# LayerNorm scaling of 32 token blocks moved from GpSimd to VectorE, with smaller presets, in a transformer layer whose engine queues a planner orders

## The chip, the core and the metric

The kernel runs on one core of one Trainium2 chip. The core's engines work in parallel, each through its own queue, strictly in order: TensorE (PE: matmul, with its weight load shown as PEld), VectorE (DVE), ScalarE (ACT), GpSimd (POOL) and SyncE (SP, which here only issues DMAs). An instruction starts when all semaphores that it waits for have come and the instruction ahead of it on its engine has gone. The metric is the device time of one execution in microseconds (us); lower is better.

## The reference

One pre-LayerNorm layer on 2048 tokens of 448 features, in bfloat16. Attention looks back at 8 positions two apart; the second half is a gated MLP in which tokens are mixed by a 2048 by 2048 matrix.

```python
def _A_ref(x, wqkv, wo):                 # 16 heads of 28, window 8, dilation 2
    q, k, v = split(x @ wqkv)
    idx = pos[:, None] - arange(8) * 2   # earlier positions; idx < 0 is masked
    attn = softmax(where(mask, q . k[idx] * 28 ** -0.5, -1e9))
    return (attn . v[idx]).reshape(B, S, D) @ wo
def _B_ref(x, w_in, w_sp, b_sp, w_out):
    z = gelu(x @ w_in)                   # 1792 wide
    z1, z2 = z[..., :896], layernorm(z[..., 896:])
    g = einsum('ts,bsf->btf', w_sp, z2) + b_sp
    return (z1 * g) @ w_out
h  = x + _A_ref(layernorm(x), wqkv, wo)
h2 = h + _B_ref(layernorm(h), w_in, w_sp, b_sp, w_out)
```

## The kernel before

The work is a graph of small tasks. A task names an engine (or two to choose from), an assumed duration in us, the buffers that it reads and writes, and a priority. `Graph.schedule` runs a list scheduler over the graph when the kernel is built: it always takes the engine that can start a ready task soonest, and there the task of the best priority. What comes out is a fixed order for each engine's queue; `Sched` then adds the semaphore waits. So an assumed duration never delays anything on the chip by itself. It decides where a task stands in its queue, and on which of two engines a copy out of PSUM lands.

Tokens are handled in 16 blocks of 128 (`m`); attention in 18 blocks of 114 queries (`i`). The stages that matter here:

- `layernorm(m, 0)` for the 16 blocks of x, and `layernorm(m, 1)` for the 16 blocks of h: DVE takes statistics (`bn_stats` L486, `bn_aggr` L488), POOL makes the reciprocal deviation in two one-column instructions (`va`, L512, and the power `rstd`, L514, both in `rstd_of`), POOL scales the 128x448 block into the ring `tring` (L491), PE transposes it with four matmuls (L496), and ACT or DVE copies the result into `xhT` (L508 or L509, both in `copy_on`).
- `qk_tile`: query and key projections, 32 tiles of four matmuls (L524). `att_block`: V projection (L535), logits (L547), exponential on ACT (L556), mask on DVE (L564), attention times V (L569), normalisation on DVE (L575, L577), transposition (L582). `y_block`: output projection (L596) and residual add on DVE (L599).
- The MLP: z2 tiles (L632), their GELU (ACT, L637), a LayerNorm of 896 columns with statistics and scaling on DVE (L640, L642, L645) and `rstd_of` on POOL; then z1 tiles (L654), the token mixing (L667) and the output (L685).

At the start POOL presets constants: the ring `V1` (4 slots, L424), whose column 28 of each head has to hold 1, and the ring `E` (3 slots, L426), whose columns past the queries are read by L569. POOL also copies the key weights (L475), PE runs 28 warm-up matmuls (L479), and DVE makes the attention mask (L429 to L434).

Of the kernel before, what the change touches and what calls it, by code (L numbers as in the profile page):

```python
# [9 lines left out]
DH = 28  # L10
F_DIM = 1792
FH = 896
EPS = 1e-5
# [4 lines left out]
NQ = 114  # L18
# [6 lines left out]
F32 = mybir.dt.float32  # L25
I32 = mybir.dt.int32
ALU = mybir.AluOpType
# [270 lines left out]
def bass_sequential_preLN__sliding_local_dilated__mixer_gmlp__prompt_kernel(  # L298
# [13 lines left out]
    G = Graph()  # L312

    with contextlib.ExitStack() as top:
        def sb(name, shape, dt):
            return top.enter_context(nc.sbuf_tensor(name, shape, dt))

        NTR, NST, NV, NE, NOT, NU = 4, 4, 4, 3, 2, 3
        x_tm = sb("x_tm", [128, NB, D], BF16)
        tring = sb("tring", [128, NTR, D], BF16)  # L320
# [5 lines left out]
        mhalf = sb("mhalf", [128, 1], F32)  # L326
        st = sb("st", [128, NST, 12], F32)
        mv = sb("mv", [128, 3 * NB, 2], F32)
        va = sb("va", [128, 3 * NB], F32)
        rstd = sb("rstd", [128, 3 * NB], F32)  # L330
# [11 lines left out]
        V1 = sb("V1", [128, NV, NHEAD, 32], BF16)  # L342
        E = sb("E", [128, NE, NHEAD, 128], BF16)
# [32 lines left out]
        P_V = Pool("V", NV)  # L376
        P_E = Pool("E", NE)
# [12 lines left out]
        def act_us(n, sbuf=False):  # L390
            return (n + (190 if sbuf else 105)) / 1200.0

        def dve_us(n, rate=1.0):
            return (n / rate + 85) / 960.0
# [4 lines left out]
        def blocks_of(lo, hi):  # L399
# [12 lines left out]
              writes=r_wq, prio=-95)  # L412
        G.add([("pool", 0.2)], [lambda e: e.memset(wkp.rearrange("p c g (h d) -> p (c g h) d", h=4)[:, :, 28:32], 0.0)],
              writes=r_wk, prio=-94)
# [6 lines left out]
                                                          channel_multiplier=1)], reads=[r_mf], writes=[r_mf], prio=-50)  # L421
        G.add([("pool", 0.2)], [lambda e: e.iota(ij, [[1, 128]], base=0, channel_multiplier=1)], writes=[r_ij], prio=-50)
        for s in range(NV):
            G.add([("pool", 0.5)], [lambda e, s=s: e.memset(V1[:, s], 1.0)], writes=[P_V.res[s]], prio=-40)  # L424
        for s in range(NE):
            G.add([("pool", 0.9)], [lambda e, s=s: e.memset(E[:, s].bitcast(F32), 0.0)], writes=[P_E.res[s]], prio=-40)  # L426
        init_slots = {P_V: [P_V.res[s].w_task for s in range(NV)], P_E: [P_E.res[s].w_task for s in range(NE)]}
        for fn, rd, wr in (
            (lambda e: e.tensor_single_scalar(ij, ij, 1, ALU.bitwise_and), [r_ij], [r_ij]),  # L429
# [52 lines left out]
        def layernorm(m, i, prio):  # L482

            k = i * NB + m
            s = Buf(P_st)
            G.add([("dve", dve_us(D))], [lambda e: e.bn_stats(st[:, s.slot, 0:6], x_tm[:, m, :])],  # L486
                  [r_x[m]], [s], [s], prio=prio)
            G.add([("dve", 0.10)], [lambda e: e.bn_aggr(mv[:, k, :], st[:, s.slot, 0:6])], [s], [r_mv[k]], prio=prio)  # L488
            rstd_of(k, prio)
            t = Buf(P_tr)  # L490
            G.add([("pool", 0.65)], [lambda e: e.tensor_scalar(tring[:, t.slot, :], x_tm[:, m, :], mv[:, k, 0:1],  # L491
                                                              rstd[:, k:k + 1], ALU.subtract, ALU.mult)],
                  [r_x[m], r_mv[k], r_rs[k]], [t], [t], prio=prio)
            b = Buf(P_bank)
            G.add([("pe", 0.27)], [
                lambda e, c=c: e.transpose(psb[0:DC, b.slot * 1024 + c * 128: b.slot * 1024 + c * 128 + 128],  # L496
                                           tring[:, t.slot, c * DC:(c + 1) * DC], ident[:, :]) for c in range(NCH)],
                [t, r_ident], [b], [b], prio=prio)

            def evac(e):  # L500
                dst = xhT[0:DC, :, PAD + 128 * m: PAD + 128 * m + 128]
                src = psb[0:DC, b.slot * 1024: b.slot * 1024 + 512].rearrange("p (c t) -> p c t", c=NCH)
                return copy_on(e, dst, src)
            G.add([("act", act_us(512)), ("dve", dve_us(512, 2))], [evac], [b], [r_xhT[m]], prio=prio)

        def copy_on(e, dst, src):
            if hasattr(e, "activation"):
                return e.activation(dst, src, AF.Copy)  # L508
            return e.tensor_copy(dst, src)  # L509

        def rstd_of(k, prio):
            G.add([("pool", 0.2)], [lambda e: e.tensor_scalar(va[:, k:k + 1], mv[:, k, 1:2], EPS, None, ALU.add)],  # L512
                  [r_mv[k]], [r_va[k]], prio=prio)
            G.add([("pool", 0.3)], [lambda e: e.tensor_tensor(rstd[:, k:k + 1], va[:, k:k + 1], mhalf[:, 0:1], ALU.pow)],  # L514
                  [r_va[k], r_half], [r_rs[k]], prio=prio)

        def qk_tile(tc, g8, prio):
# [12 lines left out]
        def att_block(i):  # L530
# [23 lines left out]
            for hh in range(4):  # L554
# [10 lines left out]
                                          maskb[0:nk, mi:mi + 1, 0:nq].to_broadcast([nk, NHEAD, nq]), ALU.mult)],  # L565
                [ev, r_mask], [ev], prio=i - 0.6)
            ob = Buf(P_bank)
            G.add([("pe", 0.9)], [
                lambda e, g=g, hh=hh: e.matmul(psum[:, ob.slot * 512 + (4 * g + hh) * 32: ob.slot * 512 + (4 * g + hh) * 32 + DH + 1],  # L569
                                               E[0:nk, ev.slot, hh * 4 + g, :], V1[0:nk, v.slot, 4 * g + hh, 0:DH + 1])  # L570
                for g in range(4) for hh in range(4)],
# [18 lines left out]
        def y_block(m):  # L590
            lo, hi = 128 * m, 128 * m + 128
            ro = [r_OT[b] for b in range(NAB) if _att_geom(b)[0] < hi and _att_geom(b)[0] + _att_geom(b)[1] > lo]
            b = Buf(P_bank)
            p = pos(m) + 1.6
            G.add([("pe", pe_us(4, D))], [
                lambda e, c=c: e.matmul(bank(b, D), qT[0:DC, c, PAD + lo:PAD + hi], wo_sb[:, c, :],  # L596
                                        start=(c == 0), stop=(c == NCH - 1)) for c in range(NCH)],
                ro + [r_wo], [b], [b], prio=p)
            G.add([("dve", dve_us(D))], [lambda e: e.tensor_tensor(x_tm[:, m, :], bank(b, D), x_tm[:, m, :], ALU.add)],  # L599
                  [b, r_x[m]], [r_x[m]], prio=p)  # L600
            layernorm(m, 1, p + 0.3)
# [6 lines left out]
        for m in range(NB):  # L608
            layernorm(m, 0, pos(m) - 7.0)
# [5 lines left out]
        for i in range(NAB):  # L615
            att_block(i)
            t0, nq, nk = _att_geom(i)
            while next_y < NB and (i == NAB - 1 or 128 * next_y + 128 <= t0 + nq - PAD):
                y_block(next_y)
                next_y += 1  # L620
# [4 lines left out]
        for m in range(NB):  # L625
            k = 2 * NB + m
            s = Buf(P_st)
# [129 lines left out]
```

## Time and profile before

| | |
|---|---|
| Time, median of 3 runs | 301.98 us (301.05 to 302.22) |
| The profiled execution: its own time, its span | 302.17 us, 300.5 us |
| PE busy, share of the span | 268.0 us, 89% |
| DVE busy | 153.1 us, 51% |
| ACT busy | 102.2 us, 34% |
| POOL busy | 111.9 us, 37% |
| Mean granted TensorE clock | 0.953 |

Busy time is the time in which an engine's instructions ran. Instructions of an engine overlap a little at their ends, so busy time can pass the time that went by. The span goes from the first to the last instruction that the profile shows; the time of an execution holds a little more than its span. The granted clock is a share of 2.4 GHz: 0.5 is 1.2 GHz throughout.

### The profile page before, as it was taken

What the parts mean: (1) busy time and instruction counts of PE and PEld (TensorE: products, weight loads), DVE (VectorE), ACT (ScalarE), POOL (GpSimd) and SP (SyncE); (2) the same over time, 40 slices, a digit from 0 to 9 for tenths busy, and PEclk for the clock granted to TensorE, in tenths of its full rate; (3) what the DMA queues carried; (4) which work ended last, traced back from release to release, by engine and by line L of the source; (5) the groups of instructions that cost most, each with busy time, mean ns of one, the idle gap of its engine ahead of it and who ended that gap; (6) DMA issues with size and microseconds to landing.
All of it is one profiled execution on the core that took longest, in us unless ns stands there. A gap on an engine that the chain in (4) does not pass through costs nothing.

```text
span 300.5 us, 4652 instructions
## 1 busy us (share of the span) xinstructions
PE 268.0 (89%) x1868; PEld 133.9 (45%) x1868; DVE 153.1 (51%) x321; ACT 102.2 (34%) x193; POOL 111.9 (37%) x155
## 2 busy tenths in 40 slices
PE   7489894997797869878999999999999999999995
PEld 2144452553463445534544444444444444444442
DVE  6861593693795767777996222322133122322223
ACT  1236773564684564545760110010100111011000
POOL 9999999858635353386443000000000000000000
PEclk9879998799999965899999999999999999999999
DMA  7999450000000001222200003443034520000001
GB/s 174 301 260 215 99 87 1 2 2 0 0 2 2 2 17 37 53 52 51 53 21 2 0 0 55 98 96 97 0 83 97 101 65 0 31 33 0 0 2 61
DMA packets 42182, 16.91 MB, mean 56 GB/s; under 512 B 35248, under 2 KB 41584, under 8 KB 42160
## 3 DMA queue, kind: packets, MB, share of 16 engines
q1 hardware_dynamic: 42160, 16.61, 23.7%
q8 instruction: 15, 0.25, 0.3%
q14 instruction: 7, 0.06, 0.1%
HBM read 6.37 MB, written 1.84 MB: 27 GB/s over the span
## 4 chain that ended last, share of the span: by engine, by line
PE 55%; POOL 29%; DVE 9%; DMA 2%; issue 2%; ACT 0%; DVEq 0%; SPq 0%; POOLq 0%
PE psum L667 31%; POOL tring L491 18%; POOL rstd L514 8%; PE psum L654 7%; PE psum L685 7%; POOL va L512 3%; PE psum L596 3%; DVE st L640 2%; PE psum L496 2%; DMA early<-in_A_wqkv_dram 2%; PE psum L524 2%; DVE z2p L645 2%; DVE st L486 1%; PE psum L547 1%; DVE x_tm L599 1%
## 5 line engine op out<-in xcount | busy, mean ns | idle before, releaser
L491 POOL TENSOR_SCALAR tring<-x_tm,mv,rstd 128x448 bf16<-128x448 bf16 x32 | 63.5, 1988 | 3.8 <-PE psum L496 2.8
L672 DVE TENSOR_TENSOR ub<-psum,bb 128x512 bf16<-128x512 f32 x28 | 19.4, 691 | 83.8 <-PE psum L667 83.8
L659 ACT ACTIVATE z1p<-psum 128x512 bf16<-128x512 f32 x28 | 16.7, 597 | 114.8 <-PE psum L654 114.8
L667 PE MATMUL psum<-wsp,z2p 128*128 128x512 bf16 x224 | 51.2, 379 | 0.5 <-DVE z2p L645 0.5
L667 PE MATMUL psum<-early,z2p 128*128 128x512 bf16 x224 | 50.8, 379 | 0.0
L556 ACT ACTIVATE E<-psum 128x456 bf16<-128x456 f32 (+1 forms) x72 | 34.4, 557 | 14.8 <-PE psum L547 14.7
L496 PE MATMUL psum<-ident,tring 128*112 128x128 bf16 x128 | 15.2, 250 | 25.3 <-POOL tring L491 25.3
L667 PEld LDWEIGHTS psum<-wsp,z2p 128*128 128x128 bf16 x224 | 21.8, 98 | 27.2 <-DVE z2p L645 0.9
L667 PEld LDWEIGHTS psum<-early,z2p 128*128 128x128 bf16 x224 | 21.9, 98 | 26.4
L524 PE MATMUL psum<-xhT,early 112*128 112x512 bf16 x128 | 31.1, 379 | 0.0
L514 POOL TENSOR_TENSOR rstd<-va,mhalf 128x1 f32<-128x1 f32 x48 | 28.8, 610 | 1.4
L654 PE MATMUL psum<-xhT,w_in 112*128 112x512 bf16 x112 | 28.8, 378 | 0.0
L512 POOL TENSOR_SCALAR va<-mv 128x1 f32<-128x1 f32 x48 | 11.1, 244 | 43.4 <-DVE mv L488 31.1
L496 PEld LDWEIGHTS psum<-ident,tring 128*112 128x112 bf16 x128 | 11.4, 149 | 33.8 <-POOL tring L491 32.0
L632 PE MATMUL psum<-w_in,xhT 112*128 112x448 bf16 x128 | 26.0, 360 | 0.0
L509 DVE COPY xhT<-psum 112x512 bf16<-112x512 bf16 x19 | 7.9, 420 | 28.3 <-PE psum L496 28.3
L685 PE MATMUL psum<-w_out,z1p 128*128 128x448 bf16 x112 | 21.8, 352 | 0.0
L637 ACT ACTIVATE z2p<-psum 128x448 bf16<-128x448 f32 x32 | 17.3, 543 | 10.9 <-PE psum L632 10.9
L564 DVE TENSOR_TENSOR E<-E,maskb 128x1824 bf16<-128x1824 bf16 (+1 forms) x18 | 19.6, 1094 | 0.3 <-ACT E L556 0.2
L486 DVE BATCH_NORM_STATS2 st<-x_tm 128x6 f32<-128x448 bf16 x32 | 18.9, 611 | 1.3 <-DMA x_tm<-in_A_x_dram 1.0
L535 PE MATMUL psum<-early,xhT 112*128 112x448 bf16 (+1 forms) x72 | 19.2, 404 | 0.0
L640 DVE BATCH_NORM_STATS2 st<-z2p 128x6 f32<-128x448 bf16 x32 | 17.9, 600 | 0.0
(59 smaller groups left out, 261.0 us busy)
## 6 DMA issues: line engine op xcount, KB each, us to landing
out_dram<-tring SPq DMA_DIRECT2D x16, 112.0 KB, 1.8
w_in<-in_B_w_in_dram SPq DMA_DIRECT2D x1, 1568.0 KB, 14.0
x_tm<-in_A_x_dram SPq DMA_DIRECT2D x1, 896.0 KB, 10.5
early<-in_A_wqkv_dram SPq DMA_DIRECT2D x1, 784.0 KB, 6.2
w_out<-in_B_w_out_dram SPq DMA_DIRECT2D x1, 784.0 KB, 14.6
bb<-in_B_b_sp_dram SPq DMA_DIRECT2D x1, 512.0 KB, 13.3
wsp<-in_B_w_sp_dram SPq DMA_TRANSPOSE x32, 2.8
early<-in_B_w_sp_dram SPq DMA_TRANSPOSE x32, 2.6
```

The lines of the kernel that those rows point to most:

```text
L486: G.add([("dve", dve_us(D))], [lambda e: e.bn_stats(st[:, s.slot, 0:6], x_tm[:, m, :])], [r_x[m]], [s], [s], prio=prio)
L491: G.add([("pool", 0.65)], [lambda e: e.tensor_scalar(tring[:, t.slot, :], x_tm[:, m, :], mv[:, k, 0:1], rstd[:, k:k + 1], ALU.subtract, AL ...
L496: lambda e, c=c: e.transpose(psb[0:DC, b.slot * 1024 + c * 128: b.slot * 1024 + c * 128 + 128], tring[:, t.slot, c * DC:(c + 1) * DC], ide ...
L512: G.add([("pool", 0.2)], [lambda e: e.tensor_scalar(va[:, k:k + 1], mv[:, k, 1:2], EPS, None, ALU.add)], [r_mv[k]], [r_va[k]], prio=prio)
L514: G.add([("pool", 0.3)], [lambda e: e.tensor_tensor(rstd[:, k:k + 1], va[:, k:k + 1], mhalf[:, 0:1], ALU.pow)], [r_va[k], r_half], [r_rs[k ...
L524: lambda e, c=c: e.matmul(bank(b, 512), wsrc[:, c, gg, :], xhT[0:DC, c, col0:col0 + 512], start=(c == 0), stop=(c == NCH - 1)) for c in ra ...
L556: lambda e, hh=hh: e.activation(E[0:nk, ev.slot, hh * 4:(hh + 1) * 4, 0:nq], bank(lb[hh], 512, 0, nk).rearrange("p (g c) -> p g c", c=128) ...
L632: lambda e, c=c, b=b, h=h, m=m: e.matmul(bank(b, D), xhT[0:DC, c, PAD + 128 * m: PAD + 128 * m + 128], w_in[:, c, FH + D * h: FH + D * (h ...
L640: lambda e, h=h, m=m, s=s: e.bn_stats(st[:, s.slot, 6 * h:6 * h + 6], z2p[:, m, D * h:D * (h + 1)])],
L654: lambda e, c=c: e.matmul(bank(b, 512), w_in[:, c, fc * 128:(fc + 1) * 128], xhT[0:DC, c, PAD + 512 * tc: PAD + 512 * (tc + 1)], start=(c ...
L667: lambda e, s=s: e.matmul(bank(b, 512), z2p[:, s, fc * 128:(fc + 1) * 128], w[:, s, :], start=(s == 0), stop=(s == NB - 1)) for s in range ...
L685: lambda e, f=f: e.matmul(bank(b, D), z1p[:, f, 128 * m:128 * m + 128], w_out[:, f, :], start=(f == 0), stop=(f == FC7 - 1)) for f in rang ...
```

## The change

The 32 scalings at L491 go to DVE, with 0.32 us assumed for each. The assumed durations of the two `rstd` instructions and of attention times V (L569) get other numbers. The V ring is preset only in column 28 of each head, the E ring only in the columns from 110 on. Since the planner places everything again, the whole front part of the program is reordered.

```diff
         for s in range(NV):
-            G.add([("pool", 0.5)], [lambda e, s=s: e.memset(V1[:, s], 1.0)], writes=[P_V.res[s]], prio=-40)
+            G.add([("pool", 0.2)], [lambda e, s=s: e.memset(V1[:, s, :, DH:DH + 1], 1.0)], writes=[P_V.res[s]], prio=-40)
         for s in range(NE):
-            G.add([("pool", 0.9)], [lambda e, s=s: e.memset(E[:, s].bitcast(F32), 0.0)], writes=[P_E.res[s]], prio=-40)
+            G.add([("pool", 0.3)], [lambda e, s=s: e.memset(E[:, s, :, NQ - 4:], 0.0)], writes=[P_E.res[s]], prio=-40)
...
-            G.add([("pool", 0.65)], [lambda e: e.tensor_scalar(tring[:, t.slot, :], x_tm[:, m, :], mv[:, k, 0:1],
+            G.add([("dve", 0.32)], [lambda e: e.tensor_scalar(tring[:, t.slot, :], x_tm[:, m, :], mv[:, k, 0:1],
                                                               rstd[:, k:k + 1], ALU.subtract, ALU.mult)],
...
-            G.add([("pool", 0.2)], [lambda e: e.tensor_scalar(va[:, k:k + 1], mv[:, k, 1:2], EPS, None, ALU.add)],
+            G.add([("pool", 0.24)], [lambda e: e.tensor_scalar(va[:, k:k + 1], mv[:, k, 1:2], EPS, None, ALU.add)],
...
-            G.add([("pool", 0.3)], [lambda e: e.tensor_tensor(rstd[:, k:k + 1], va[:, k:k + 1], mhalf[:, 0:1], ALU.pow)],
+            G.add([("pool", 0.61)], [lambda e: e.tensor_tensor(rstd[:, k:k + 1], va[:, k:k + 1], mhalf[:, 0:1], ALU.pow)],
...
-            G.add([("pe", 0.9)], [
+            G.add([("pe", 0.43)], [
                 lambda e, g=g, hh=hh: e.matmul(psum[:, ob.slot * 512 + (4 * g + hh) * 32: ob.slot * 512 + (4 * g + hh) * 32 + DH + 1],
```

POOL's queue at the start of the program, as a difference (`va` and `rstd` are the one-column instructions, `early` is the key weights):

```order
-L424 MEMSET V 128x512 x3
-L426 MEMSET E 128x1024 x3
+L424 MEMSET V 128x16 x3
+L426 MEMSET E 128x16x18 x3
+L512 TENSOR_SCALAR va<-mv 128x1 x2
+L514 TENSOR_TENSOR rstd<-va,mhalf 128x1 x2
 L475 COPY early<-early 112x16x28 x4
 L512 TENSOR_SCALAR va<-mv 128x1 x2
 L514 TENSOR_TENSOR rstd<-va,mhalf 128x1 x2
-L491 TENSOR_SCALAR tring<-x_tm,mv,rstd 128x448 x2
```

The first two blocks' `rstd` now stand ahead of the copies of the key weights, and no scaling stands on POOL any more.

PE's queue behind the warm-up, before (L496 transposes a scaled block, L535 is V, L524 queries and keys, L547 logits):

```order
L496 MATMUL psum<-ident,tring 112x128 x8
L535 MATMUL psum<-early,xhT 128x448 x8
L496 MATMUL psum<-ident,tring 112x128 x8
L535 MATMUL psum<-early,xhT 128x448 x4
L524 MATMUL psum<-xhT,early 128x512 x16
L496 MATMUL psum<-ident,tring 112x128 x4
L524 MATMUL psum<-xhT,early 128x512 x16
L496 MATMUL psum<-ident,tring 112x128 x12
L535 MATMUL psum<-early,xhT 128x448 x4
L547 MATMUL psum<-qT,kT 128x114 x16
```

The same place now:

```order
L496 MATMUL psum<-ident,tring 112x128 x8
L535 MATMUL psum<-early,xhT 128x448 x8
L496 MATMUL psum<-ident,tring 112x128 x4
L535 MATMUL psum<-early,xhT 128x448 x4
L496 MATMUL psum<-ident,tring 112x128 x8
L524 MATMUL psum<-xhT,early 128x512 x32
L496 MATMUL psum<-ident,tring 112x128 x12
L535 MATMUL psum<-early,xhT 128x448 x4
L547 MATMUL psum<-qT,kT 128x114 x16
```

The instructions up to the first logits are the same in number; the eight query and key tiles now stand together, and the fourth and fifth block are transposed ahead of them.

DVE's queue late in the attention part, before (L486 and L488 are a block's statistics, L599 the residual add):

```order
L599 TENSOR_TENSOR x_tm<-psum,x_tm 128x448
L577 TENSOR_TENSOR otm<-psum,rcp 114x448
L486 BN_STATS st<-x_tm 128x6
L575 RECIPROCAL rcp<-psum 114x16
L488 BN_AGGR mv<-st 128x2
L509 COPY qT<-psum 112x4x114
L577 TENSOR_TENSOR otm<-psum,rcp 114x448
L564 TENSOR_TENSOR E<-E,maskb 128x16x114
```

The corresponding place now:

```order
L599 TENSOR_TENSOR x_tm<-psum,x_tm 128x448
L577 TENSOR_TENSOR otm<-psum,rcp 114x448
L486 BN_STATS st<-x_tm 128x6
L575 RECIPROCAL rcp<-psum 114x16
L488 BN_AGGR mv<-st 128x2
L577 TENSOR_TENSOR otm<-psum,rcp 114x448
L564 TENSOR_TENSOR E<-E,maskb 128x16x114
L491 TENSOR_SCALAR tring<-x_tm,mv,rstd 128x448
```

The scaling now stands in DVE's own queue, two larger instructions behind the `bn_aggr` whose result POOL has to turn into `rstd` for it.

## Rows read from the trace of the kernel before

**Rows 1.** Busy time by engine in stretches: instructions, granted clock, DMA share, GB/s

```profile
109.00:122.00 13.00, 10.86 (x123) 6.89 (x122) 9.07 (x16) 7.11 (x16) 5.79 (x6) 0.51 0.18 42
137.00:162.00 25.00, 24.55 (x127) 12.07 (x125) 22.76 (x56) 14.88 (x27) 11.75 (x30) 1.00 0.14 32
0.00:137.00 137.00, 108.17 (x1105) 59.57 (x1106) 89.90 (x193) 72.36 (x141) 100.12 (x126) 0.90 0.31 73
```

**Rows 2.** Who waited for whom: us in total, times, longest

```profile
PE psum L496 <- POOL tring L491: 25.3, 18, 4.0
...
DVE z2p L645 <- POOL rstd L514: 2.8, 2, 1.9
```

**Rows 3.** Groups of instructions, shapes kept apart: busy us, mean ns

```profile
L491 POOL TENSOR_SCALAR tring<-x_tm,mv,rstd 128x448 bf16<-128x448 bf16 x32 | 63.5, 1988 | 3.8 <-PE psum L496 2.8
...
L645 DVE TENSOR_SCALAR z2p<-z2p,mv,rstd 128x896 bf16<-128x896 bf16 x16 | 8.1, 506 | 3.4 <-POOL rstd L514 2.8
...
L509 DVE COPY xhT<-psum 112x512 bf16<-112x512 bf16 x19 | 7.9, 420 | 28.3 <-PE psum L496 28.3
...
L509 DVE CAST V<-psum 128x448 bf16<-128x448 f32 x8 | 4.8, 610 | 2.2 <-PE psum L535 2.2
```

**Rows 4.** Timeline of PE, consecutive starts in a dense stretch: start, us

```profile
63.41 0.38 PE L547 MATMUL psum<-qT,kT 32*128 32x114 bf16 x16
63.72 1.04 PE L524 MATMUL psum<-xhT,early 112*128 112x512 bf16 x4
64.59 0.92 PE L596 MATMUL psum<-wo,qT 112*128 112x448 bf16 x4
65.35 1.03 PE L524 MATMUL psum<-xhT,early 112*128 112x512 bf16 x4
...
66.42 0.39 PE L496 MATMUL psum<-ident,tring 128*112 128x128 bf16 x4
66.64 1.89 PE L524 MATMUL psum<-xhT,early 112*128 112x512 bf16 x8
```

**Rows 5.** The chain that ended last, one piece of attention times V

```profile
62.69 0.39 PE psum L569 x16
```

**Rows 6.** Timeline of PE at the start and at the last transposition

```profile
2.13 7.98 PE L479 MATMUL psum<-warm,ident 128*128 128x512 bf16 x28 [2.13 <-POOL ident L406]
13.55 0.68 PE L496 MATMUL psum<-ident,tring 128*112 128x128 bf16 x4 [3.44 <-POOL tring L491]
...
21.69 3.63 PE L524 MATMUL psum<-xhT,early 112*128 112x512 bf16 x16
...
31.99 0.38 PE L547 MATMUL psum<-qT,kT 32*128 32x114 bf16 x16
...
136.93 17.57 PE L632 MATMUL psum<-w_in,xhT 112*128 112x448 bf16 x92
```

**Rows 7.** Timeline of POOL at the start: start, us

```profile
5.14 2.74 POOL L426 MEMSET E<- 128x1024 f32 x3
8.00 2.20 POOL L475 COPY early<-early 112x448 bf16<-112x448 bf16 x4
...
10.53 1.09 POOL L514 TENSOR_TENSOR rstd<-va,mhalf 128x1 f32<-128x1 f32 x2
```

**Rows 8.** Timeline of DVE at the start: start, us

```profile
4.59 3.36 DVE L430 CAST z2p<-z2p 128x128 f32<-128x128 int32 x1
...
9.31 0.11 DVE L434 MEMSET maskb<- 14x64 uint32 x1
```

**Rows 9.** Timeline, DVE instructions that ran beside POOL's power

```profile
36.48 1.11 DVE L564 TENSOR_TENSOR E<-E,maskb 128x1824 bf16<-128x1824 bf16 x1
...
142.51 1.08 DVE L645 TENSOR_SCALAR z2p<-z2p,mv,rstd 128x896 bf16<-128x896 bf16 x2
```

**Rows 10.** Timeline of POOL, the same two places

```profile
35.98 2.02 POOL L514 TENSOR_TENSOR rstd<-va,mhalf 128x1 f32<-128x1 f32 x2
...
141.87 1.17 POOL L514 TENSOR_TENSOR rstd<-va,mhalf 128x1 f32<-128x1 f32 x2
```

## The prediction

> **What bounds the kernel now.** I first read busy time by stretches. Up to 137 us no engine is full: PE is busy for 108 us, POOL for 100, DVE for 90, ACT for 72 [rows 1]. After that PE runs without a gap worth naming: the last transposition of a normalised block is followed at 136.93 by 92 z2 matmuls in a row [rows 6], and in 137 to 162 PE is busy for 24.55 of 25 us [rows 1]. The change touches nothing behind that point but its queue order. So the question is when the last L496 runs.
>
> Next, how much PE work stands ahead of it. Consecutive starts give what a task costs PE at full clock [rows 4]: a transposition of four 0.22 us (66.42 to 66.64), four matmuls of 512 columns 0.87, four of 448 columns 0.76, a block's logits 0.31; attention times V is 0.39 [rows 5]. The program has 32 + 18 transpositions (11.0), 32 query and key tiles (27.8), 18 V and 16 output tiles (25.8), 18 logits (5.6) and 18 products with V (7.0): 77.2 us, plus 9 z2 tiles at 0.76 that now run ahead of the last transposition: 84.0. From the first transposition at 13.55 to 136.93 [rows 6], 123.4 us pass. 39.4 of them are no work.
>
> The list of waits says what most of that is: PE sat idle 25.3 us, 18 times, for the scaling L491 on POOL [rows 2]. One scaling takes POOL 1.988 us [rows 3], where the planner assumed 0.65; it therefore put the transpositions into PE's queue too early, and everything behind them stands still. The other 14 us are smaller waits and stretches at a lower clock: in 109 to 122 PE was granted 0.51 of its speed, that is 1.2 GHz [rows 1].
>
> **The change, part by part.** *Off POOL:* 32 scalings, 63.5 us [rows 3]. What PE waits for through them is removed as far as nothing else is late.
>
> *Onto DVE:* 32 scalings of 448 columns. The trace has no such instruction on DVE. Nearest is L645, the same operation with the same kinds of operand on 896 columns: 506 ns [rows 3]. Half the columns cannot cost more than that, and not less than half of it: 0.25 to 0.51 us, 8.1 to 16.2 us in all. I take 0.39, near the middle, since a part of an instruction's time does not shrink with its columns: 12.5 us. The Trainium skill ("VectorE: DVE Perf Modes", side-by-side cycle account) puts such an operation in its four-elements-a-cycle mode at about 158 fixed cycles; that makes an estimate of 0.28 us, 9.0 us in all, and a span 3.4 us shorter than mine.
>
> *Off DVE again:* the planner now gives ACT more of the PSUM copies. By the order, DVE keeps 13 of 19 `xhT` copies and 7 of 9 V copies, which are 6 x 0.42 + 2 x 0.61 = 3.7 us [rows 3], and 3 others fewer, some 0.5 each by the same rows: 5.2 us together. DVE's busy time up to the last scaling goes from 89.9 to 89.9 + 12.5 - 5.2 = 97.2.
>
> *The presets* cost POOL less, but by themselves bring nothing: the E presets end at 7.88, and the copies of the key weights that follow start at 8.00 [rows 7], so their input sets the start. What counts is that two `rstd` pairs now fit in ahead of those copies; a pair of powers takes 1.09 [rows 7], and between nothing and all of the 2.74 us of the E presets alone becomes free. The mask work on DVE ends at 9.42, with a cast of 3.36 us in it [rows 8] that ran beside the presets; it may become shorter by anything from 0 to 3 us, and I count 0, because PE's warm-up keeps PE until 10.11 anyway [rows 6].
>
> *The start.* DVE scales the first two blocks at 9.4 to 10.2 instead of POOL behind its copies and powers. PE transposes them at about 10.2 to 11. The next two blocks' statistics are on DVE until 11.6, their `rstd` on POOL until about 13 (behind the copies, which end at 10.2). DVE copies the first two out by 12.3; two V tiles follow on PE at half speed until 15.3; then transposition, copy, scaling and transposition of blocks 3 to 5 in turn, some 2.5 us, so that the query and key tiles begin at about 17.8 (21.69 before). Eight of them (7.0), three transpositions and a V tile later the first logits run at 26.2, not 31.99 [rows 6].
>
> *From there to the last transposition.* PE has 12 instead of 9 z2 tiles ahead, 86.3 us of work, of which 11.8 are done by 26.2: 74.5 are left, so not before 100.7. DVE sets more: in 137 to 162, where it waited 2.8 us [rows 2], its 22.76 busy us filled 22.2, a factor of 1.03. 97.2 busy us so fill 94.4. To these come its idle times: 2.9 before its first instruction (the sum of 89.9 starts there too), some 4 in the chain of the start above, and one in ten of the 84 us after 26, 8.5. That tenth is my choice; the bounds are nothing (101.3, where PE stands too) and what DVE was idle before without the scaling: 137 - 87.3 - 25.3 = 24.4 in all, which ends at 118.8. My value is 94.4 + 15.4 = 109.8.
>
> *After it.* From 136.93 to 300.5 are 163.6 us. 12 z2 matmuls are now ahead, at 17.57 / 92 = 0.19 each [rows 6]: 161.3 remain. POOL's `rstd` for z2 and DVE's part there are as before.
>
> Sum: 109.8 + 161.3 = 271.1 us of span, against 300.5; 29.4 less. The profiled execution took 302.17, 0.2 above the median, and 1.7 more than its span. That makes **273 us**.
>
> **The rivals.**
>
> *The scaling waits in DVE's own queue (slower).* A scaling on POOL that waited for its `rstd` held up only POOL. On DVE it holds up the mask, the normalisation of attention, the residual add and the copies into `xhT`, and PE waits for all of these. Price: a power takes 0.55 alone, and beside the mask L564 far longer: a pair took 2.02 instead of 1.09 us [rows 7, 9, 10]; for `va` the change's own 0.24 may stand. If each of the 32 scalings waits 1.24 us (0.24 and a power of 1.0), DVE ends 40 us later, at 149.5: span 311, time 312. It decides at 29.4 / 32 = 0.92 us of wait per scaling. For it: DVE has waited for `rstd` before, 1.4 us each in two cases [rows 2]. Against it: late in the queue there now stand L577 and L564, some 1.7 us, between `bn_aggr` and scaling, as the last two pieces of order show. Chance 0.05.
>
> *DVE becomes the bound with the waits it had.* ACT's copies, PE and DVE hand blocks to each other, and a queue 89% full has little room to catch up. If its idle time after the start is two to four times what I take, the last transposition comes at 119 to 137, in the middle 128: span 289, time 291. For it: even with POOL as the brake DVE was busy for 66% of the front. Chance 0.14.
>
> *DVE and POOL exclude each other.* If a scaling on DVE and a power on POOL cannot run at the same time, the worst case is one power of 0.55 for each scaling on DVE's path, 18 us: last transposition at 128, time 291. The mask shows such an effect on POOL's side (2.02 instead of 1.09); but the pair of L645, from 142.51 on, ran beside a pair of powers until 143.04, took 1.08 and left the powers at 1.17 [rows 9, 10]. So the likely payer is POOL, by 0.1 us. The Trainium skill ("SBUF — State Buffer", section Who interferes with whom) has the rule: a VectorE instruction in a two-port mode and a GpSimd instruction take an exclusive lock for the whole instruction, and the later one blocks. By that rule one of the two in 142.5 to 143.0 would have grown by up to 0.5 us; the trace shows 0.1. Chance 0.04.
>
> *It does not do what it says.* If the 25.3 us were only where the waiting shows, and PE next waits as long for the `xhT` copies or for banks, the end stays within 1.5 us of 302. Speaking against it, PE's work is 84 of 123 us and no other wait of PE comes near 25 us. Chance 0.04.
>
> **How the numbers follow.** Forecast, 264 to 282 (the ends of the idle bounds: 101.3 + 161.3 + 1.7 and 118.8 + 161.3 + 1.7): 0.68. Better than 264, by a cheaper scaling and no idle time: 0.05. Waits kept: 0.14; exclusion: 0.04; no effect: 0.04; slower: 0.05. 0.5%, 1.5 us, is about what a measurement of this kernel can tell from no change. Faster by more: 0.68 + 0.05 + 0.14 + 0.04 = 0.91; within it 0.04; slower 0.05. For 8 in 10 the range takes the forecast and the better part of the two rivals around 291: 264 to 290.
>
> **What the profile of the changed kernel would show.** L491 on DVE at 0.25 to 0.51 us. First query and key tile near 17.8, first logits near 26, last L496 between 101 and 119, then 161 us to the end. PE's wait for `tring` down from 25.3 to under 8; DVE busy some 97 us up to the last scaling, with no wait for `rstd` beyond some 5 us in all. The prediction is wrong if the list of waits has a new one above 15 us: DVE for POOL's power (the first rival), or PE for DVE's copies (the second); if L491 or the powers grow far beyond these means (the third); or if the half clock of 109 to 122 comes back elsewhere for longer than 13 us.

## The result, and the profile of the changed kernel

The changed kernel took 265.34 us (median of 4 runs, 264.80 to 268.68); the kernel before took 301.89 beside it (301.05 to 302.22). The ratio is 0.8816, 95% interval 0.8741 to 0.8892: 12% faster. The forecast was 273, range 264 to 290. The profiled execution took 264.8 us with a span of 263.0, so the span is 37.5 us shorter than the 300.5 of before.

I read the changed kernel in the order in which I read the one before. First busy time by engine in stretches, cut at the last transposition (102.15) as [rows 1] were cut at 137: PE, its weight loads, DVE, ACT, POOL, then granted clock, DMA share, GB/s.

```profile
0.00:102.00 102.00, 97.30 (x1112) 56.16 (x1113) 89.26 (x212) 78.04 (x155) 34.53 (x93) 1.00 0.45 94
102.00:126.00 24.00, 24.00 (x126) 12.01 (x125) 22.78 (x59) 13.33 (x25) 12.08 (x30) 1.00 0.27 50
```

PE is now busy for 97.30 of 102 us where it was busy for 108 of 137, and POOL fell from 100.12 to 34.53. PE is nearest to its limit in the front, with DVE at 88% close behind. Of the 35 us between 137 and 102, PE's idle time gives 24.1 (28.83 became 4.70) and its busy time 10.9. By the prediction's prices there is no less work ahead of the cut than before (86.3 us against 84.0). What did change is the clock that PE was granted, a mean of 0.90 up to 137 [rows 1] and 1.00 now; a tenth of 137 us makes an estimate of at most 14 us for it. The second row is the stretch that answers to 137 to 162 in [rows 1], and looks the same.

The waits, in us, times and longest:

```profile
DVE st L486 <- DMA x_tm<-in_A_x_dram: 2.5, 2, 2.1
...
DVE tring L491 <- POOL rstd L514: 1.8, 4, 0.7
...
DVE z2p L645 <- POOL rstd L514: 0.8, 1, 0.8
...
PE psum L496 <- DVE tring L491: 0.2, 1, 0.2
```

The 25.3 us of [rows 2] are 0.2, and no new wait takes their place: DVE waits 1.8 us for `rstd` ahead of scalings, in four places. Only the first row is of any size, a wait for the third and fourth block of x.

The groups that answer to [rows 3], busy us and mean ns:

```profile
L491 DVE TENSOR_SCALAR tring<-x_tm,mv,rstd 128x448 bf16<-128x448 bf16 x32 | 11.9, 379 | 2.0 <-POOL rstd L514 1.8
...
L645 DVE TENSOR_SCALAR z2p<-z2p,mv,rstd 128x896 bf16<-128x896 bf16 x16 | 8.0, 502 | 0.8 <-POOL rstd L514 0.8
...
L509 DVE COPY xhT<-psum 112x512 bf16<-112x512 bf16 x13 | 5.2, 416 | 0.8 <-PE psum L496 0.6
...
L509 DVE CAST V<-psum 128x448 bf16<-128x448 f32 x7 | 4.2, 616 | 0.4 <-PE psum L535 0.2
```

A scaling went from 1988 ns to 379. It has half the columns of L645 and takes three quarters of its time.

PE's timeline at the places of [rows 6]: start, us, and in brackets the idle time ahead with what ended it.

```profile
9.51 0.61 PE L496 MATMUL psum<-ident,tring 128*112 128x128 bf16 x8
...
10.41 1.69 PE L535 MATMUL psum<-early,xhT 112*128 112x448 bf16 x8 [0.30 <-DVE xhT L509]
...
14.76 7.07 PE L524 MATMUL psum<-xhT,early 112*128 112x512 bf16 x32
...
23.19 0.38 PE L547 MATMUL psum<-qT,kT 32*128 32x114 bf16 x16
...
102.15 0.39 PE L496 MATMUL psum<-ident,tring 128*112 128x128 bf16 x4
...
102.38 15.30 PE L632 MATMUL psum<-w_in,xhT 112*128 112x448 bf16 x80
```

In the kernel before the last transposition started at 136.66, just ahead of the 136.93 of [rows 6]:

```profile
136.66 0.43 PE L496 MATMUL psum<-ident,tring 128*112 128x128 bf16 x4 [1.43 <-POOL tring L491]
```

These starts split the 37.5 us: 8.8 of them are won by the first logits (31.99 to 23.19), 25.7 from there to the last transposition (104.7 us became 79.0), and 3.0 behind it (163.8 became 160.8), since 80 and not 92 z2 matmuls are left there. The clock row of the profile's page (tenths of full speed, 40 slices) has no low slice any more:

```profile
PEclk9999999999999999999999999999999999999999
```

Last, the start on DVE and POOL, which answers to [rows 7, 8]:

```profile
4.36 0.22 DVE L430 CAST z2p<-z2p 128x128 f32<-128x128 int32 x1
...
5.55 0.11 DVE L434 MEMSET maskb<- 14x64 uint32 x1
5.59 0.80 DVE L491 TENSOR_SCALAR tring<-x_tm,mv,rstd 128x448 bf16<-128x448 bf16 x2
```

```profile
3.53 0.97 POOL L426 MEMSET E<- 128x288 bf16 x3
...
4.87 1.09 POOL L514 TENSOR_TENSOR rstd<-va,mhalf 128x1 f32<-128x1 f32 x2
...
7.74 2.06 POOL L475 COPY early<-early 112x448 bf16<-112x448 bf16 x4 [1.78 <-DMA early<-in_A_wqkv_dram]
```

With the small presets POOL has `rstd` of the first two blocks by 5.96, ahead of the weight copies instead of behind them. And the cast L430, 3.36 us before, takes 0.22: the mask is done at 5.66, not 9.42, and DVE scales the first blocks at once.

### The profile page after: what moved, and what is told of

The parts are those of the page before. It is cut to its first block, busy times and chain, and to the rows that moved or that the text cites. A ratio compares the mean times of both kernels' runs of the same rounds, so it can differ in the third digit from the quotient of the medians.

```text
span 263.0 us, 4647 instructions
## 1 busy us (share of the span) xinstructions
PE 255.1 (97%) x1868; PEld 129.8 (49%) x1868; DVE 152.4 (58%) x342; ACT 106.3 (40%) x204; POOL 46.6 (18%) x123
## 4 chain that ended last, share of the span: by engine, by line
PE 89%; DMA 3%; DVE 3%; ACT 2%; SPq 1%; POOL 1%; issue 0%; DVEq 0%
PE psum L667 37%; PE psum L524 10%; PE psum L632 9%; PE psum L654 9%; PE psum L685 8%; PE psum L596 4%; PE psum L535 4%; DMA x_tm<-in_A_x_dram 3%; PE psum L496 2%; PE psum L569 2%; PE psum L547 2%; ACT E L556 2%; PE psum L582 1%; DVE st L486 1%; DVE tring L491 1%; SPq L440 0%
## 5 line engine op out<-in xcount | busy, mean ns | idle before, releaser
L556 ACT ACTIVATE E<-psum 128x456 bf16<-128x456 f32 (+1 forms) x72 | 35.0, 562 | 1.4 <-PE psum L547 1.2
L524 PE MATMUL psum<-xhT,early 112*128 112x512 bf16 x128 | 30.5, 379 | 0.1
L514 POOL TENSOR_TENSOR rstd<-va,mhalf 128x1 f32<-128x1 f32 x48 | 27.7, 580 | 3.2
L512 POOL TENSOR_SCALAR va<-mv 128x1 f32<-128x1 f32 x48 | 13.2, 283 | 72.8 <-DVE mv L488 62.0
L486 DVE BATCH_NORM_STATS2 st<-x_tm 128x6 f32<-128x448 bf16 x32 | 19.2, 610 | 2.6 <-DMA x_tm<-in_A_x_dram 2.5
L637 ACT ACTIVATE z2p<-psum 128x448 bf16<-128x448 f32 x32 | 17.1, 544 | 7.2 <-PE psum L632 7.2
L654 PEld LDWEIGHTS psum<-xhT,w_in 112*128 112x128 bf16 x112 | 10.9, 97 | 13.3
L524 PEld LDWEIGHTS psum<-xhT,early 112*128 112x128 bf16 x128 | 11.5, 97 | 12.0 <-ACT V L508 0.2
L632 PEld LDWEIGHTS psum<-w_in,xhT 112*128 112x128 bf16 x128 | 12.1, 98 | 10.3
L535 PE MATMUL psum<-early,xhT 112*128 112x448 bf16 (+1 forms) x72 | 16.1, 352 | 0.8 <-DVE xhT L509 0.8
L685 PEld LDWEIGHTS psum<-w_out,z1p 128*128 128x128 bf16 x112 | 11.0, 98 | 10.4
## 6 DMA issues: line engine op xcount, KB each, us to landing
w_out<-in_B_w_out_dram SPq DMA_DIRECT2D x1, 784.0 KB, 15.5
```

Of the source, the lines that this page charges most:

```text
L514: G.add([("pool", 0.61)], [lambda e: e.tensor_tensor(rstd[:, k:k + 1], va[:, k:k + 1], mhalf[:, 0:1], ALU.pow)], [r_va[k], r_half], [r_rs[ ...
L524: lambda e, c=c: e.matmul(bank(b, 512), wsrc[:, c, gg, :], xhT[0:DC, c, col0:col0 + 512], start=(c == 0), stop=(c == NCH - 1)) for c in ra ...
L535: lambda e, c=c: e.matmul(bank(b, D, 0, nk), xhT[0:DC, c, t0:t0 + nk], stg[:, c, 2 * D:3 * D], start=(c == 0), stop=(c == NCH - 1)) for c ...
L556: lambda e, hh=hh: e.activation(E[0:nk, ev.slot, hh * 4:(hh + 1) * 4, 0:nq], bank(lb[hh], 512, 0, nk).rearrange("p (g c) -> p g c", c=128) ...
L632: lambda e, c=c, b=b, h=h, m=m: e.matmul(bank(b, D), xhT[0:DC, c, PAD + 128 * m: PAD + 128 * m + 128], w_in[:, c, FH + D * h: FH + D * (h ...
L654: lambda e, c=c: e.matmul(bank(b, 512), w_in[:, c, fc * 128:(fc + 1) * 128], xhT[0:DC, c, PAD + 512 * tc: PAD + 512 * (tc + 1)], start=(c ...
```

## The experiments

The change has three parts: which engine scales, what the planner is told that it costs (and so the order on all engines), and the presets. My theory when I began: the engine removes the wait, the order follows the true cost, the presets help little or only through the start. Its rival: it is the order, and the engine matters little. Each kernel has 4 runs and is compared with the kernel before on the same chip; the places are from its profile. The chips differ: the kernel before took 302.04 us beside p1 to p4, 303.41 beside p5 to p8 and 303.07 beside p9 to p11. A difference in us between rows of two chips carries this; the ratios do not. "First tile" and "first logits" are PE's first L524 and L547, "wait" is PE's for the scaled block.

| kernel | us | ratio to before (95%) | first tile | first logits | last L496 | wait |
|---|---|---|---|---|---|---|
| before | 301.89 | 1 | 21.69 | 31.99 | 136.66 | 25.3 |
| changed | 265.34 | .8816 (.8741 to .8892) | 14.76 | 23.19 | 102.15 | 0.2 |
| p1_presets | 299.29 | .9884 (.9827 to .9941) | 18.27 | 28.60 | 133.55 | 22.7 |
| p2_move | 270.98 | .8937 (.8866 to .9007) | 18.73 | 27.39 | 108.94 | 2.4 |
| p3_costs | 278.05 | .9183 (.9127 to .9238) | 24.45 | 35.65 | 120.37 | 4.8 |
| p7_costs_presets | 274.72 | .9072 (.9041 to .9103) | 21.16 | 31.27 | 115.99 | 2.4 |
| p4_oldplan | 277.34 | .9155 (.9104 to .9206) | 19.42 | 28.08 | 110.80 | 5.7 |
| p11_oldplan_presets | 277.34 | .9126 (.9057 to .9196) | 19.77 | 28.43 | 111.14 | 6.1 |
| p6_newplan_pool | 288.16 | .9502 (.9469 to .9534) | 20.33 | 31.11 | 125.91 | 15.5 |
| p5_twice | 270.01 | .8925 (.8886 to .8963) | 15.64 | 24.07 | 107.06 | 1.7 |
| p10_newcosts | 266.14 | .8759 (.8703 to .8815) | 14.17 | 22.83 | 104.29 | 0.6 |
| p8_xfirst | 266.49 | .8792 (.8742 to .8841) | 13.52 | 21.96 | 102.04 | 1.0 |
| p9_poolstream | 280.67 | .9235 (.9162 to .9307) | 17.21 | 27.28 | 118.84 | 3.0 |

### p1: the presets alone

The kernel before, with only the change's two preset lines:

```diff
-G.add([("pool", 0.5)], [... e.memset(V1[:, s], 1.0)] ...
+G.add([("pool", 0.2)], [... e.memset(V1[:, s, :, DH:DH + 1], 1.0)] ...
-G.add([("pool", 0.9)], [... e.memset(E[:, s].bitcast(F32), 0.0)] ...
+G.add([("pool", 0.3)], [... e.memset(E[:, s, :, NQ - 4:], 0.0)] ...
```

> The kernel before with the smaller presets alone (V ring column 28, E ring columns from 110; their assumed durations too), scaling still on GpSimd. Theory (two separate gains, one at the start and one in the middle; the presets matter only at the start): GpSimd is the brake from 8 to 62 us, so what it saves before 8.0 us, at most 3.3 us of presets, is gained once: 298.5 to 300.5. The mask cast at L430 falls from 3.36 us to below 1, since nothing on GpSimd runs beside it. Rival (the prediction's own: presets bring nothing by themselves, because the key weights set the start at 8.0): 301.5 to 302.5. Rival (the presets are most of the start's 8.8 us): 294 or less.

299.29 us, 1.2% less. POOL's timeline shows that more than memsets became shorter: `rstd` and even a scaling now run ahead of the weight copies, which start where they started ([rows 7], 8.00).

```profile
4.87 1.08 POOL L514 TENSOR_TENSOR rstd<-va,mhalf 128x1 f32<-128x1 f32 x2
5.96 1.88 POOL L491 TENSOR_SCALAR tring<-x_tm,mv,rstd 128x448 bf16<-128x448 bf16 x1
8.05 2.06 POOL L475 COPY early<-early 112x448 bf16<-112x448 bf16 x4 [0.21 <-DMA early<-in_A_wqkv_dram]
```

The first tile comes 3.4 us earlier, and 3.1 are kept up to the last transposition. PE's wait is still 22.7 us.

### p2: everything but the presets

The changed kernel with those two lines as they were before.

> The changed kernel with the old large presets (and their old assumed durations): the move to VectorE and the new assumed durations alone. Theory: first logits some 3 us later than in the changed kernel (23.2 to about 26), since rstd of the first two blocks stands behind presets until 7.9 and copies until 10.2 and the cast at L430 takes 3.4 us again; the middle as in the changed kernel: 267 to 270. Rival (the presets carry nothing): 264.5 to 266. Rival (VectorE and GpSimd exclude each other more widely): 272 or more.

270.98 us, just outside the theory's window: without the presets the change brings 5.6 us less. By the medians that is more than p1's 2.7, but the intervals of the two ratios overlap (0.8866 to 0.9007 and 0.8741 to 0.8892), so that it is more is not shown. DVE's timeline has the long cast again, and it ends when the presets do:

```profile
4.37 3.60 DVE L430 CAST z2p<-z2p 128x128 f32<-128x128 int32 x1
```

Part of the 5.6 may be another thing: in this profile the mean granted clock was 0.981, with some slices below full speed that the changed kernel does not have.

### p3 and p7: the right costs, scaling left on POOL

p3 is the kernel before, with its presets, told what four of its tasks take: the scaling, the two `rstd` instructions (0.24 and 0.61) and attention times V (0.43, assumed as 0.9 before). p7 is the changed kernel, which has the last three numbers and the small presets, with the scaling on POOL. The scaling's line, against the kernel before:

```diff
-G.add([("pool", 0.65)], [lambda e: e.tensor_scalar(tring[:, t.slot, :], ...
+G.add([("pool", 1.99)], [lambda e: e.tensor_scalar(tring[:, t.slot, :], ...
```

> Old presets, scaling on GpSimd as before, but with the assumed durations that the profile of before shows (1.99 us for the scaling, 0.24, 0.61, and 0.43 for attention times V): only the order changes. Theory (the speed of the scaling's engine counts as well as the order): GpSimd needs 32 x 2.84 = 91 us for the normalisations, from 10 us on, and these cannot be spread evenly, so 278 to 292. Rival (only the wrong place in TensorE's queue did harm): 266 to 272. Rival (order does nothing): 300 to 303.

> Scaling on GpSimd with the measured durations assumed for it, and the small presets: the changed kernel in all but the engine. Theory (presets are worth the more the more the start is the brake; GpSimd is busy from 8 us on): 3 to 6 us under the 278 us of the same with large presets, 272 to 275; what remains to 265.3, some 8 us, is the engine's own share. Rival (the gains do not add): 277 to 279.

278.05 and 274.72 us. With the scaling left on POOL, truer numbers in the plan bring 24 us. No run tells how much of that is the scaling's number and how much the other three's. The waits and the groups of p3 show that the scaling is as slow as ever, and that PE waits for it 4.8 us instead of 25.3:

```profile
PE psum L496 <- POOL tring L491: 4.8, 3, 3.1
```

```profile
L491 POOL TENSOR_SCALAR tring<-x_tm,mv,rstd 128x448 bf16<-128x448 bf16 x32 | 66.5, 2080 | 2.0 <-PE psum L496 0.9
```

The planner now puts other work of PE ahead of a transposition whose block is late: 68 z2 matmuls run ahead of the last transposition where it had been 36, and 60 are left behind it. The planner also places copies anew: DVE has 17 of the 32 `xhT` copies instead of 19. Between p7 and the changed kernel only the engine and its number differ, with the order that follows from them: 9.4 us by the medians, 7.7 by the ratios.

### p4 and p11: the engine alone, in the old order

The plan of before is made with POOL at 0.65; only then do the 32 scalings change engine, each in its old place. p11 has the small presets besides, in the same order.

```diff
 order = G.schedule()
+for t in scales:
+    t.eng = "dve"
```

> The kernel before, planned exactly as before (TensorE's and ScalarE's queues unchanged, presets unchanged), but the 32 scalings are issued to VectorE at the place in the program that the plan gave them on GpSimd. Only the engine changes. Theory: the old order assumed 1.15 us for va, rstd and scaling together; on VectorE they take about 1.24, so TensorE's transpositions fit where they stand and its wait for tring falls below 5 us; VectorE's queue was not planned for it, so some waits for rstd of 0.5 us each remain: 270 to 280. Rival (the new order is what brings the gain): 288 or more. Rival (the engine alone brings all): 264 to 268.

> The small presets, everything planned as before (the old assumed durations of the presets too, so the order is unchanged), the 32 scalings issued to VectorE. Theory (the presets are worth the more the less GpSimd brakes behind the start; 2.7 us with scaling on GpSimd and the old plan, 5.6 us in the changed kernel): 272 to 275. Rival (with the old order rstd stands behind the key weight copies, so the presets bring nothing): 276.5 to 278.

Both 277.34 us. The engine alone brings 25 us, and the order made with the change's numbers 12 more by the medians, 9 by the ratios (p11 against the changed kernel, which differ in nothing but what the planner placed). PE still waits 5.7 us in p4, where the theory had less than 5. The old order puts a scaling where DVE has other work: the first runs at 13.08, behind three blocks' statistics, though POOL was through with the first two `rstd` at 11.49.

```profile
PE psum L498 <- DVE tring L493: 5.7, 6, 2.6
...
DVE tring L493 <- POOL rstd L516: 0.4, 1, 0.4
```

In p11 the presets bring nothing that the runs can tell (ratios of 0.9155 and 0.9126, with intervals that overlap). POOL is through with them early and then stands idle, because in the old order `rstd` is behind the copies:

```profile
8.27 2.06 POOL L475 COPY early<-early 112x448 bf16<-112x448 bf16 x4 [3.77 <-DMA early<-in_A_wqkv_dram]
10.30 0.39 POOL L514 TENSOR_SCALAR va<-mv 128x1 f32<-128x1 f32 x2
```

So the presets' worth depends on the order: about 0 with `rstd` behind the copies, 2.7 to 5.6 us where the planner may move it ahead.

### p6: the new order, scaling on POOL

The changed kernel's plan, made with DVE at 0.32, and then `t.eng = "pool"` for the 32 scalings.

> The changed kernel, planned exactly as changed (TensorE's and ScalarE's queues and presets), but the 32 scalings are issued to GpSimd, where one takes 2 us, at the place in the program that the plan gave them on VectorE. Theory (what costs is that the plan expects a scaled block in 0.32 us and gets it after 2 us and more): TensorE's wait for tring comes back to 20 us or more, 288 to 305. Rival (the order or VectorE's queue brings the gain, the engine does not matter): 265 to 275.

288.16 us: the total is at the lower end of the theory's window, the wait is outside it, 15.5 instead of 20 or more:

```profile
PE psum L498 <- POOL tring L493: 15.5, 15, 2.9
```

The order for a fast scaling, run with a slow one, is 11 us better than the old order (p1, 299.3), which assumed 0.65. It is 13 us worse than the order made for the slow one (p7).

### p5: every scaling twice

The changed kernel, in which each scaling is first written to a spare buffer that nobody reads, and then to its place; the plan does not know of it. It puts DVE's load where the prediction put it.

```diff
-[lambda e: e.tensor_scalar(tring[:, t.slot, :], x_tm[:, m, :], ...)]
+[lambda e, dst=dst: e.tensor_scalar(dst(), x_tm[:, m, :], ...)
+ for dst in (lambda: ub[:, twice["u"], 0:D], lambda: tring[:, t.slot, :])]
```

> The changed kernel with every LayerNorm scaling done twice on VectorE, the first time into a spare buffer; all queues otherwise in the order of the changed kernel. VectorE gets 32 x 0.3 to 0.38 = 10 to 12 us more. Theory (VectorE sets the end of the front together with TensorE: it was busy 89 of 102 us): 6 to 11 us of it come through, 271 to 276. Rival (TensorE alone is the bound, VectorE has room): 265 to 268. Rival (VectorE's waits multiply): over 280.

270.01 us, between both. DVE was given 12.1 us more, and 4.7 came through (3.3 by the ratios):

```profile
L494 DVE TENSOR_SCALAR ub<-x_tm,mv,rstd 128x448 bf16<-128x448 bf16 x32 | 12.1, 378 | 1.8 <-POOL rstd L518 1.8
```

By stretches (columns as above), to its last transposition at 107.06:

```profile
0.00:107.00 107.00, 100.13 (x1112) 56.80 (x1112) 97.25 (x243) 78.72 (x155) 35.37 (x93) 0.98 0.42 91
```

DVE is busy for 97.25 us, the prediction's 97.2. That is 8.0 more than in the changed kernel, not 12.1, since a stretch's busy time counts a moment once and the extra scalings overlap their neighbours. DVE is neither the sole bound, or all 8 would have come through, nor hidden. The clock has a part too: in 80 to 107 the mean granted clock was 0.94, which makes an estimate of at most 1.6 us of PE's time:

```profile
80.00:107.00 27.00, 25.25 (x280) 14.83 (x278) 25.95 (x63) 20.91 (x42) 6.26 (x16) 0.94 0.21 41
```

### p10: the costs measured in the changed kernel

```diff
-("dve", 0.32) ... ("pool", 0.24) ... ("pool", 0.61)
+("dve", 0.39) ... ("pool", 0.28) ... ("pool", 0.58)
```

> The changed kernel planned with the durations that its own profile shows: 0.39 for the scaling, 0.28 and 0.58 for the two rstd instructions. Theory (TensorE has 86 us of work between 9.5 and 102.2 us, so at most some 6 us are left to any order): 263 to 267, not to be told from the changed kernel. Rival (the plan still decides several us): 260 or less, or 269 or more.

266.14 us, which the runs cannot tell from the changed kernel. Errors of this size (0.32 for 0.38) cost nothing measurable; the four wrong numbers of p3, among them 0.65 for 1.99, cost 24 us.

### p8: blocks 3 and 4 of x loaded first

The largest wait left in DVE's front is for x. Here that load goes out ahead of the weights for queries and keys:

```diff
-dma(lambda e: e.dma_start(stg[:, :, 0:2 * D], ...), 802, ..., prio=-99.985)
+dma(lambda e: e.dma_start(stg[:, :, 0:2 * D], ...), 1500, ..., prio=-99.975)
```

> The changed kernel with the load of token blocks 3 and 4 ahead of the query and key weights, and 1500 instead of 802 assumed for those weights, so that rstd of blocks 3 and 4 stands ahead of the key weight copies. Theory (the start waits for these blocks: VectorE idle 2.1 us for their load until 8.48, and query and key tiles from 14.76): the tiles begin at 12 to 13, 262 to 264. Rival (the start is not on the path, since VectorE and TensorE are full later on): 264.5 to 266.

266.49 us, no gain; the theory's 262 to 264 is missed. PE's timeline: the tiles begin 1.2 us earlier, and the last transposition runs where it ran.

```profile
13.52 3.63 PE L524 MATMUL psum<-xhT,early 112*128 112x512 bf16 x16
...
102.04 0.39 PE L496 MATMUL psum<-ident,tring 128*112 128x128 bf16 x4
```

This earlier start was worth nothing by itself: in the changed kernel PE has 86.3 us of work from 9.5 us on ahead of that transposition, and starts it 92.6 us later.

### p9: POOL kept as busy as before

The changed kernel, with a useless scaling of a constant tile on POOL behind each true one on DVE; nobody reads it. POOL is about as loaded as in the kernel before (106.3 us busy, 111.9 there), and runs beside DVE.

```diff
+if t in scales:
+    n = scales.index(t) % NU
+    sch.issue("pool", [lambda e, n=n: e.tensor_scalar(ub[:, n, 0:D], warm[:, 0:D],
+                       mhalf[:, 0:1], mhalf[:, 0:1], ALU.subtract, ALU.mult)], ...)
```

> The changed kernel with GpSimd kept as busy as before: behind each scaling in the program GpSimd scales a constant tile into a spare buffer nobody reads, 32 x 2 us. All other queues in the order of the changed kernel. Theory (VectorE's SBUF-to-SBUF work is held up while GpSimd streams, as the cast at L430 was by the presets): the scaling L491 on VectorE grows from 0.38 to 0.8 us or more on average, and since rstd also queues behind the extra work, 280 to 300 in all. Rival (no exclusion; only rstd is late): L491 stays within 0.36 to 0.42 us, 270 to 285. Rival (neither matters): 265 to 267.

280.67 us. The mean scaling grew from 379 to 542 ns, between what the two theories gave, and the wait for `rstd` from 1.8 us to 11.8:

```profile
L493 DVE TENSOR_SCALAR tring<-x_tm,mv,rstd 128x448 bf16<-128x448 bf16 x32 | 17.1, 542 | 11.9 <-POOL rstd L516 11.8
```

One place shows the two engines side by side, DVE first and then POOL:

```profile
63.81 0.79 DVE L493 TENSOR_SCALAR tring<-x_tm,mv,rstd 128x448 bf16<-128x448 bf16 x1 [0.24 <-POOL rstd L516]
```

```profile
63.77 1.87 POOL L720 TENSOR_SCALAR ub<-warm,mhalf 128x448 bf16<-128x448 bf16 x1
```

Started 0.04 us behind POOL's, DVE's scaling takes twice its 0.38 us, and is through a microsecond before POOL's. The Trainium skill ("SBUF — State Buffer", section Who interferes with whom) says that a VectorE instruction in a two-port mode and a GpSimd instruction shut each other out for the whole instruction; if it applies to this instruction, DVE's could not have ended ahead of POOL's 65.64, and the trace shows 64.60.

Nor was it slowed evenly. How long a scaling takes depends on when it starts beside POOL's (DVE first, then POOL):

```profile
13.89 0.39 DVE L493 TENSOR_SCALAR tring<-x_tm,mv,rstd 128x448 bf16<-128x448 bf16 x1
...
21.24 0.74 DVE L493 TENSOR_SCALAR tring<-x_tm,mv,rstd 128x448 bf16<-128x448 bf16 x1
```

```profile
13.12 1.87 POOL L720 TENSOR_SCALAR ub<-warm,mhalf 128x448 bf16<-128x448 bf16 x1
...
21.15 1.88 POOL L720 TENSOR_SCALAR ub<-warm,mhalf 128x448 bf16<-128x448 bf16 x1
```

The 13 scalings that started up to 0.29 us behind a start of POOL's ended 0.83 to 0.84 us behind that start, whenever they began (21.98 against 21.15; 64.60 against 63.77). The six that started 0.44 to 0.84 us behind it took 0.39, as if alone. Two that started 1.25 and 1.29 us behind it took 0.76 and 0.71. So a scaling was held in parts of POOL's 1.87 us and ran at its own speed in the rest; with 0.38 us for itself, the first hold ends about 0.45 us into POOL's instruction, an estimate from these ends.

The scalings took 5.2 us more of DVE's time (17.1 for 11.9). How much of the 15 us comes from late `rstd`, how much from the held scalings and how much from the clock (0.93 up to 119) stays open.

## Why the prediction was right, and where its sum was off

**The cause.** Right: the wait for the scaling was 25.3 us and is 0.2. That it was wrongly planned, "put the transpositions into PE's queue too early", was a subordinate clause of mine, and it is half the story. With the large presets, before takes 302.0, the plan with truer costs alone 278.05 (p3), the engine alone 277.34 (p4), both 270.98 (p2). Either brings 24 to 25 us, both bring 31. They are largely substitutes: a slow scaling does little harm if PE has other work ahead of it, and a wrong order does little if the scaling is short. The rival "it is the order, the engine matters little" is wrong as well, since the engine brings 8 to 9 us with measured costs on both sides (p7). Which of the plan's four numbers counts was not tried apart. Part of each gain may be the clock: its mean over the span was 0.953 before, 0.967 in p3, 0.994 in p4 and 1.000 in the changed kernel, so that 14, 9, 2 and 0 us are the most that it can have cost, estimates from these clocks and spans.

**L491 on DVE.** Taken as 0.39 between bounds of 0.25 and 0.51; 0.379. The fixed part that I assumed is there: half the columns of L645 take three quarters of its time. The estimate of 0.28 from the Trainium skill ("VectorE: DVE Perf Modes", side-by-side cycle account) was too low.

**Copies.** DVE's `xhT` and V copies were to fall by 3.7 us, with others by 5.2. L509 on DVE fell by 5.4 in all (21.7 to 16.3).

**DVE's busy time: the step that failed.** 97.2 were forecast up to the last scaling, 89.26 are busy up to 102. Of the 7.9, 3.9 are the mask work L429 to L433 (5.24 before, 1.36 after), 3.1 of them the cast L430: "it may become shorter by anything from 0 to 3 us, and I count 0". My reason, PE's warm-up, was no reason: my sum counts all of DVE's work up to the last scaling, wherever it stands. The scalings gave 0.6, the copies 0.2. Of the other 3.2, some 2.6 are overlap. A stretch's busy time counts a moment once, even where two instructions overlap at their ends, and cannot pass the time that went by, though my note under the first table says so. The durations of DVE's instructions up to 137 add to 100.9 us before, for 89.9 busy, and up to 102 to 102.9 now, for 89.3. I had added whole scalings to a busy time that was counted so.

The factor of 1.03 was a misreading of the same kind: 22.76 busy us cannot fill 22.2. The first of the two waits that make the 2.8 us began ahead of 137, and only 0.55 of its 1.85 lies in the stretch:

```profile
137.55 1.10 DVE L645 TENSOR_SCALAR z2p<-z2p,mv,rstd 128x896 bf16<-128x896 bf16 x2 [1.85 <-POOL rstd L514]
```

The factor took 2.8 us off the sum, about what the overlap would have, so two slips cancel, by luck. What my sum then has is 94.4 busy and 15.4 idle; up to 102.0 there are 89.3 and 12.7. So of the 7.8 us by which my 109.8 was too late, 5.1 are DVE's load and 2.7 its idle time. p5 agrees, though its load is spread in another way: with DVE at 97.25 the last transposition came at 107.06, not 109.8, and the time was 270.0, not 273. That "DVE sets more" than PE is not borne out: PE, busy for 97.30 of the 102 us, is nearer to its limit, though p5 shows that DVE's load counts beside it.

**The presets "by themselves bring nothing".** Wrong as a statement on the kernel before (p1: 2.7 us), right only if the order is kept (p11). I looked at the instruction that follows in the old queue, the weight copies, and not at what the planner would put there, though I had named the two `rstd` pairs.

**The start.** First tile 17.8 forecast, 14.76 measured; first logits 26.2 and 23.19. DVE scaled at 5.59, not 9.4, and the two V tiles ran in 1.69 us at full clock where I had allowed 3.0 at half speed. But p8 shows that 1.2 us of start are lost again by 102, so the start matters less than I gave it.

**Behind the last transposition.** 161.3 forecast from the z2 matmuls behind it on, 160.6 measured (102.38 to 263.0).

**The rivals.** DVE waiting in its own queue for `rstd`: 1.8 us and 0.8, forecast up to 5, and nowhere near 0.92 for each scaling. p9 shows that the mechanism is real where POOL is loaded: 11.8 us. DVE with the waits it had: its idle time was 12.7 us in all, below the forecast's. Exclusion: the powers do not hold L491, since four scalings that started 0.03 to 0.04 us behind a power (from 13.76 to 17.76 us) took 0.38 each. POOL's own scalings do (p9, up to 0.80), and the change takes these off POOL. No effect: excluded. The half clock of 109 to 122 did not come back.

## What to carry to other kernels

Where a planner sets the order, compare its assumed durations with the measured means first: four wrong ones, the largest of them wrong by a factor of three, together cost as much here as the slow engine itself, and correcting a number is one line. Judge a shorter instruction at the head of a queue by what can move into the gap and by what other engines do during it, not by the next instruction in the old order. When a brake goes, count anew how much work the next engine has: with PE busy for 97.3 of 102 us, an earlier start brought nothing.

## What the runs showed of the hardware

A cast on DVE from int32 to f32, 128 x 128, takes 0.22 us, and 3.36 to 3.60 us while POOL writes its large presets; it ends when they do, in p2 as in the kernel before. With small presets it is short (p1, the changed kernel). The rule of the Trainium skill ("SBUF — State Buffer", section Who interferes with whom) agrees with the trace in that the cast is held while POOL's instructions run; it was held over several of them in a row. A scaling on DVE beside a scaling on POOL was held only for parts of it: it took up to 0.80 us instead of 0.38, and did not wait for the end of POOL's 1.87 us (p9). What sets the cast apart from the scaling was not tried.

The clock: PE was granted full speed in every slice of the changed kernel, where the kernel before had a stretch at 0.51 of it [rows 1], after PE had stood idle again and again (in 92 to 109 us it was busy for 13.92 of 17). Kernels between the two have lower slices (mean 0.967 to 0.994 in p2 to p7). That waits removed bring part of their gain through the clock fits all of these, but no run changes the clock alone.
